# Sink values of the attention kept for all 128 rows, and their matmuls widened from 32 rows to 128

## The chip, the cores and the metric

The kernel runs on one core of one Trainium2 chip. The metric is the device time of one execution in microseconds (us); lower is better.

## The reference

The reference is a sliding-window attention with sink keys, followed by a feed-forward block. Sizes are 4 batches, 8 heads, 768 positions, head dimension 64, 4 sinks, window 128; then 3072 tokens, model width 512, feed-forward width 1024. Cut to what matters:

```python
keep = is_sink | in_window                       # key is among the first 4, or within the last 128
scores = np.where(keep, q @ k.T / sqrt(64), -1e9)
a = exp(scores - max); a = a / (a.sum() + 1e-9)
x = a @ v                                        # heads side by side: 3072 x 512
h = x @ w_in
solu = h * softmax(h)
ln = (solu - mean) / sqrt(var + 1e-6) * g_ln
out = ln @ w_out
```

## The kernel before, in words

Work goes by chunks of 128 queries: 6 chunks for a batch, 24 in all (`n` is the chunk, `c = n % 6` its place in the batch). Every float32 value is split into a high and a low part of a type (fp32r) that one pass of TensorE carries, so products are sums of two or three matmuls.

For each chunk the heads go in two blocks of 4 (`hb`) or in 4 pairs (`pr`). `turn_q`, `turn_k` (L415) transpose queries and keys on TensorE; `score` (L457, L458) makes the scores `s` of one head in two matmuls, in PSUM buffers of a pool with two (tag `s`, shared with those transposes); on VectorE `pick` (L464, COPY_PREDICATED) and `mask` (L474) take them out, `negate`, `invert` and `normalise` (L482, L494, L501) belong to the softmax; `turn_p` (L507) transposes the probabilities. `value` multiplies them with the values, pair by pair, into `acc` (shown as `av`): for each of the two heads a matmul over the chunk's own keys (L567) and one over the chunk before (L570), and, where `c` is not 0, one for the sinks of both heads (L573). There are thus 20 x 4 = 80 sink matmuls. `gather` (L580) sums the result on VectorE, `hidden` (L613) and `project` (L682) are the two feed-forward products, `turn_u` (L667) transposes between them, and `scale` (L687) and `store` write out through the buffers `ob` (two of them).

The sinks' probabilities of all 8 heads are brought together: `turn_sinks` transposes them to `skp`, whose 128 rows go by (head, high or low, sink), 16 rows a head and 32 a pair. `take_sinks` (L556) copies them twice to `skt`, once with the odd heads' rows set to zero and once with the even heads' rows, by the 0/1 columns `even` and `odd`. The sinks' values come once a batch into `vsraw` in the same order of rows; `sink_values` (L401 to L407, VectorE) splits them into high and low and puts them, in either order, in `vsink`. The sink matmul of pair `pr` takes rows 32*pr to 32*pr+31 of `vsink` (weights) and of `skt` (moving, 2 x 128 columns).

The order on every engine is fixed by a table, `PLAN`: for each step a number in sixteenths of a chunk's time. All steps of all chunks are sorted by `16*n + number` and issued in that order, each engine taking its own. `PLAN_W` does the same for the weights, which are split while the first chunks run. In the lists of order below, names end in the batch or chunk, then block or pair, then a serial number.

Of the kernel before, what the change touches and what calls it, by code (L numbers as in the profile page):

```python
# [10 lines left out]
F32 = mybir.dt.float32  # L11
F32R = mybir.dt.float32r
I32 = mybir.dt.int32
AF = mybir.ActivationFunctionType
ALU = mybir.AluOpType
# [31 lines left out]
    "sinks_lo": (-14.95, -12.0),  # L47
    "v_hi": (-31.65, -20.95),
    "v_lo": (-20.9, -18.8),
    "sink_values": (-34.95,),  # L50
    "turn_sinks": (-10.8,),
    "take_sinks": (-10.6,),
    "value": (-8.9, -8.2, -4.25, -1.4),
# [49 lines left out]
P = 128  # L103
# [39 lines left out]


def _outside(nc, consts, n_f, w_f):
    """Whether the two scalars leave the banded path's range."""
    ok = consts.tile([P, 4], F32, name="ok")
    nc.vector.tensor_scalar(ok[:, 0:1], n_f, 0.0, None, op0=ALU.is_ge)
    nc.vector.tensor_scalar(ok[:, 1:2], n_f, float(NSK), None, op0=ALU.is_le)
    nc.vector.tensor_scalar(ok[:, 2:3], w_f, 1.0, None, op0=ALU.is_ge)  # L150
    nc.vector.tensor_scalar(ok[:, 3:4], w_f, float(P), None, op0=ALU.is_le)
    allok = consts.tile([P, 1], F32, name="allok")
    nc.vector.tensor_reduce(allok, ok, axis=AX.X, op=ALU.min)
    general = consts.tile([P, 1], I32, name="general")
    nc.vector.tensor_scalar(general, allok, -1.0, 1.0, op0=ALU.mult, op1=ALU.add)
    return general


# High words of float64 whose numbers have float32's least and greatest exponent, as float32.
LEAST, MOST = struct.unpack("<2f", struct.pack("<2I", 0x38100000, 0x47EFFFFF))  # L160


def _banded(ctx, tc, q, k, v, n_sink, window, w_in, w_out, g_ln, out, val, wts):
    nc = tc.nc
    n_f, w_f = val[:, 0:1], val[:, 1:2]
    w1h, w1l, w2h, w2l = wts
    B, H, S, D = q.shape
# [3 lines left out]
    NPAIR = H // 2  # L171
# [7 lines left out]
    cpool = ctx.enter_context(tc.tile_pool(name="cpool", bufs=1))  # L179
    sb = ctx.enter_context(tc.tile_pool(name="sb", bufs=2))  # L180
# [26 lines left out]
                nc.sync.dma_start(g_sb, g_ln.rearrange("(kt p) -> p kt", p=P))  # L207

    def scalars(_, j):
        """The two int64 scalars on every partition, in float32 (exact where they can lie  # L210
        between two positions)."""
        nc.gpsimd.tensor_copy(words_f, words)
        lo, hi = words_f[:, :, 0], words_f[:, :, 1]
        nc.gpsimd.tensor_scalar(val, lo, 0.0, None, op0=ALU.is_lt)
        nc.gpsimd.tensor_tensor(val, val, hi, op=ALU.add)
        nc.gpsimd.tensor_scalar(val, val, 4294967296.0, None, op0=ALU.mult)
        nc.gpsimd.tensor_tensor(val, val, lo, op=ALU.add)

    # masks: query less key position, within a chunk (rel) and against the chunk before (rel + P)
    def at_least(out, x, lead):  # L220
        """x where lead * (partition less column) is at least (lead < 0), 0 elsewhere"""
        nc.gpsimd.affine_select(out, x, pattern=[[-lead, P]], compare_op=ALU.is_ge, fill=0.0,
                                base=-(lead < 0), channel_multiplier=lead)

# [16 lines left out]
    even = cpool.tile([P, 1], F32, name="even")  # L241
    odd = cpool.tile([P, 1], F32, name="odd")
    par = cpool.tile([P, NPAIR], F32, name="par")

    def masks(_, j):
        if j == 0:
            # a batch's first chunk
            nc.gpsimd.tensor_scalar(near, rel, w_f, None, op0=ALU.is_lt)
            at_least(near, near, 1)
            nc.gpsimd.tensor_scalar(old, ki, n_f, None, op0=ALU.is_lt)  # L250
            nc.gpsimd.tensor_copy(is_sink.rearrange("p g s -> p (g s)"), old[:, 0:NSK])
            nc.gpsimd.tensor_tensor(old, old, near, op=ALU.add)
            barred(bias0, old)
        elif j == 1:
            # the later ones
            nc.gpsimd.tensor_scalar(old, rel, float(P), w_f, op0=ALU.add, op1=ALU.is_lt)
            at_least(old, old, -1)
            nc.gpsimd.tensor_tensor(old, old, near, op=ALU.add)
            barred(bias1[:, 4:SEG], old)
            nc.gpsimd.tensor_scalar(far.rearrange("p g s -> p (g s)"), rel[:, 0:NSK], float(P), w_f,  # L260
                                    op0=ALU.add, op1=ALU.is_ge)
            nc.gpsimd.tensor_tensor(far, far, is_sink, op=ALU.mult)
            nc.gpsimd.tensor_copy(bias2[:, 4:SEG], bias1[:, 4:SEG])
            for t, bias in ((far, bias1), (is_sink, bias2)):
                barred(bias.rearrange("p (g s) -> p g s", s=4)[:, 0:SEG // 4 + 1:SEG // 4, :], t)
        else:
            ones = s_i[:, 0, :]
            nc.gpsimd.memset(ones, 1)
            at_least(m_cur, ones, 1)
            at_least(m_prev, ones, -1)  # L270
            # rows of the sink blocks go by (head, hi|lo, sink): which belong to even heads
            nc.gpsimd.memset(par, 1.0)
            nc.gpsimd.affine_select(par, par, pattern=[[-32, NPAIR]], compare_op=ALU.is_ge,
                                    fill=0.0, base=0, channel_multiplier=1)
            nc.gpsimd.affine_select(par, par, pattern=[[32, NPAIR]], compare_op=ALU.is_ge,
                                    fill=0.0, base=15, channel_multiplier=-1)
            nc.gpsimd.tensor_tensor(par[:, 0:2], par[:, 0:2], par[:, 2:4], op=ALU.add)
            nc.gpsimd.tensor_tensor(even, par[:, 0:1], par[:, 1:2], op=ALU.add)
            nc.gpsimd.tensor_scalar(odd, even, -1.0, 1.0, op0=ALU.mult, op1=ALU.add)
# [1 line left out]
    neg_half = cpool.tile([P, 1], F32, name="neg_half")  # L281
    nc.vector.memset(neg_half, -0.5)

    # weights, split into two parts that float32r products carry
    NB = 512
    blocks = [(w1h, w1l, w_in, kt, slice(i * NB, (i + 1) * NB)) for kt in range(KT1) for i in range(DFF // NB)]
    NW1 = len(blocks)
# [13 lines left out]
        bits = st["wbits", j] = sb.tile([P, NB], I32, tag=BIT_TAGS[j], name=f"wbits_{j}", bufs=2 + (BIT_TAGS[j] != "ob"))  # L301
        nc.scalar.activation(bits.bitcast(F32), raws[j][:, :, 1].bitcast(F32), AF.Abs)

    # float32 words of float64 ones: the sign and the exponent's first bit stay, the exponent's
    # other seven bits and the fraction's first 23 move up by three. What float32's exponents do
    # not reach goes to the nearest that they do.
    def least_w(_, j):
        t = st["wbits", j].bitcast(F32)
        nc.vector.tensor_scalar(t, t, LEAST, MOST, op0=ALU.max, op1=ALU.min)
# [27 lines left out]
        eng = nc.vector if j in LO_DVE else nc.gpsimd  # L337
        eng.tensor_tensor(wl[:, kt, cols], st["w", j], wh[:, kt, cols].bitcast(F32), op=ALU.subtract)  # L338

    # keys of four chunks: those at even positions of a batch before those at odd ones  # L340
    ring = cpool.tile([P, H, 4, SEG], F32R, name="ring")
    slot_of = (0, 2, 1, 3)
    st = {}
# [51 lines left out]
    def sink_values(n, _):  # L395
        b, c = divmod(n, NC)
        if c == 0:
            raw = st["vsraw", b]
            hi = sb.tile([P, D], F32R, tag="vshi", name=f"vshi_{b}", bufs=1)
            lo = sb.tile([P, D], F32R, tag="vslo", name=f"vslo_{b}", bufs=1)  # L400
            nc.vector.tensor_copy(hi, raw)  # L401
            nc.vector.tensor_tensor(lo, raw, hi.bitcast(F32), op=ALU.subtract)
            vk = sb.tile([P, 2, D], F32R, tag="vsink", name=f"vsink_{b}", bufs=2)
            tmp = sb.tile([P, 2, D], F32, tag="vstmp", name=f"vstmp_{b}", bufs=1)
            for i, (x, y) in enumerate(((hi, lo), (lo, hi))):
                nc.vector.tensor_scalar(tmp[:, i, :], y.bitcast(F32), odd, None, op0=ALU.mult)
                nc.vector.scalar_tensor_tensor(vk[:, i, :], x.bitcast(F32), even, tmp[:, i, :],  # L407
                                               op0=ALU.mult, op1=ALU.add)
            st["vsink", b] = vk

    def turn(n, hb, nm):
# [146 lines left out]
    def value(n, pr):  # L558
# [10 lines left out]
                lhs = st["vs", n - 1, hb][:, jp, 2 * x:2 * x + 2, :].rearrange("p t d -> p (t d)")  # L569
                nc.tensor.matmul(acc[:, x], lhs, pt[:, 2 * jp + x], start=False, stop=False)  # L570
        if not alone:
            rows = slice(32 * pr, 32 * pr + 32)
            nc.tensor.matmul(acc[:, :, 0, :], st["vsink", b][rows].rearrange("p t d -> p (t d)"),  # L573
                             st["skt", n][rows], start=False, stop=True)

    def gather(n, pr):
        hb, jp = divmod(pr, HB // 2)
# [9 lines left out]
        nc.sync.dma_start(ysh[D:P], y[0:D, :, 1, :])  # L587

    def tokens(n, hb):
        """x, heads side by side and tokens along the free axis."""  # L590
        y, ysh = st["y", n, hb], st["ysh", n, hb]
        xt = st["xt", n, hb] = sb.tile([P, HB // 2, P], F32, tag="xt", name=f"xt_{n}_{hb}", bufs=2)
        nc.gpsimd.tensor_tensor(xt[0:D], y[0:D, :, 0, :], ysh[0:D], op=ALU.add)  # L593
        nc.gpsimd.tensor_tensor(xt[D:P], y[D:P, :, 1, :], ysh[D:P], op=ALU.add)
# [37 lines left out]
    def solu(n, _):  # L632
# [1 line left out]
        su = sm.tile([P, 1], F32, tag="su", name=f"su_{n}")  # L634
        nc.vector.scalar_tensor_tensor(u, st["h", n], 1.0, st["e", n], op0=ALU.mult, op1=ALU.mult,
                                       accum_out=su)
        # eps times the square of the softmax's divisor: the divisor is taken into the root
        d = sm.tile([P, 1], F32, tag="d", name=f"d_{n}")
        nc.vector.tensor_scalar(d, st["se", n], EPS_SUM, None, op0=ALU.add)  # L639
        nmu = st["nmu", n] = sm.tile([P, 1], F32, tag="nmu", name=f"nmu_{n}")  # L640
# [48 lines left out]
    def store(n, _):  # L689
        nc.sync.dma_start(out[n * P:(n + 1) * P, :], st["ob", n])  # L690

    # When a chunk's steps are issued, in sixteenths of the time one chunk takes, from the
    # start of its first feed-forward product on; every engine takes its own in that order.
    stages = (load_k, load_q, load_v, k_hi, k_lo, q_hi, q_lo, turn_q, turn_k, take_q, swap_q, take_k, ring_sinks,
              score, pick, mask, negate, exps, invert, normalise, turn_p, p_hi, p_lo, part_new, part_old, sinks_hi, sinks_lo,
              v_hi, v_lo, sink_values, turn_sinks, take_sinks, value, gather, shift, tokens, x_hi, x_lo,
# [9 lines left out]


def _dense(ctx, tc, q, k, v, out, n_f, w_f, wts):
    """Any n_sink and window: every key of a sequence, in native float32 products."""
    nc = tc.nc  # L710
    B, H, S, D = q.shape
    w1h, w1l, w2h, w2l = wts
# [161 lines left out]
```

## Time and profile before

| What | Value |
|---|---|
| Time, median of 3 runs | 549.36 us (549.30 to 549.49) |
| Profiled execution, first to last instruction (span) | 547.0 us |
| Mean granted TensorE clock | 0.991 |
| Busy: TensorE matmul / weight loads | 491.5 us (90%) / 405.7 us (74%) |
| Busy: VectorE / ScalarE / GpSimd | 433.9 us (79%) / 372.3 us (68%) / 356.3 us (65%) |
| Sink matmuls (L573) | 80, from 72.0 to 518.4 us, 379 ns each |

Of the profiled execution the span is the only time that the page gives; the runs' median is 2.4 us above it. PE is TensorE's matmuls, PEld its weight loads, DVE VectorE, ACT ScalarE, POOL GpSimd, SP the engine that issues DMAs. A matmul's listed length is longer than the distance to the next one, since matmuls are pipelined: the start times tell what one costs the engine, not the lengths.

### The profile page before, as it was taken

Reading aid. Unit: us, or ns where it says so; the run is one execution under the profiler, and the core shown is the slowest. Engines: PE = TensorE matmul, PEld = TensorE weight load, DVE = VectorE, ACT = ScalarE, POOL = GpSimd, SP = SyncE. Lnnn points to the kernel's source line nnn. Section 1 sums busy time; section 2 is a strip of 40 time slices with the busy share of each in tenths; the row PEclk is TensorE's granted clock in tenths of the full one; section 3 lists DMA queues with packets and bytes.
Section 4 is the critical chain, followed back from the end, with each engine's and each line's share of the span. In section 5 each row is a group of like instructions: output and inputs, shape, how many; then the busy total and the mean of one; then the engine's idle time right before and its main releaser. Section 6 shows DMA issues by size and latency. Waiting matters only on the chain. (4 is left out here: it accounts for less than half of the span.)

```text
span 547.0 us, 9854 instructions
## 1 busy us (share of the span) xinstructions
PE 491.5 (90%) x2756; PEld 405.7 (74%) x2756; DVE 433.9 (79%) x1435; ACT 372.3 (68%) x1034; POOL 356.3 (65%) x510
## 2 busy tenths in 40 slices
PE   0046788999999999999999999999999999999995
PEld 0034566788788888888888888888888888888783
DVE  4999999986987787787887788788878878778531
ACT  3477867776676777677677677677768767755432
POOL 3967697896584677666675667667656757747520
PEclk9999898999999999999999999999999999999999
DMA  7777533343444543443444343343345343211111
GB/s 260 235 172 190 133 70 69 86 98 90 87 98 96 125 88 73 113 90 74 109 89 96 88 96 90 87 101 91 83 101 121 83 103 86 59 50 19 32 29 44
DMA packets 104205, 53.42 MB, mean 98 GB/s; under 512 B 80528, under 2 KB 92816, under 8 KB 104144
## 3 DMA queue, kind: packets, MB, share of 16 engines
q1 hardware_dynamic: 104144, 52.72, 39.9%
q8 instruction: 25, 0.41, 0.3%
q14 instruction: 36, 0.29, 0.2%
HBM read 27.53 MB, written 6.42 MB: 62 GB/s over the span
## 5 line engine op out<-in xcount | busy, mean ns | idle before, releaser
L602 POOL TENSOR_TENSOR xl<-xt,xh 128x256 fp32r<-128x256 f32 x48 | 35.5, 740 | 79.6 <-ACT xh L598 79.5
L613 PE MATMUL h<-w1h,xh 128*128 128x512 f32 x192 | 86.6, 451 | 0.2 <-DVE d L639 0.2
L489 ACT ACTIVATE sc<-sc,nmx 128x136 f32<-128x136 f32 (+1 forms) x192 | 76.3, 404 | 8.7 <-DVE nmx L482 8.7
L682 PE MATMUL o<-w2h,uh 128*128 128x512 f32 x192 | 80.1, 417 | 0.3 <-ACT uh L671 0.3
L613 PE MATMUL h<-w1l,xh 128*128 128x512 f32 x192 | 76.3, 398 | 0.2 <-DVE w1l L338 0.2
L613 PE MATMUL h<-w1h,xl 128*128 128x512 f32 x192 | 76.3, 398 | 0.0
L682 PE MATMUL o<-w2h,ul 128*128 128x512 f32 x192 | 75.7, 394 | 0.0
L682 PE MATMUL o<-w2l,uh 128*128 128x512 f32 x192 | 75.5, 393 | 0.0
L501 DVE TENSOR_SCALAR sc<-sc,rs 128x136 f32<-128x136 f32 (+1 forms) x192 | 75.3, 453 | 0.0
L580 DVE TENSOR_REDUCE y<-av 128x256 f32<-128x512 f32 x96 | 65.5, 683 | 6.2 <-PE av L573 5.8
L457 PE MATMUL s<-ring,qT 128*128 128x264 f32 (+1 forms) x192 | 57.5, 308 | 14.4 <-DVE mx L474 12.5
L522 POOL TENSOR_SCALAR_AFFINE_SELECT pc<-pt 128x1024 fp32r<-128x1024 f32 x40 | 44.5, 1111 | 23.7 <-DVE pt L515 23.7
L464 DVE COPY_PREDICATED s<-m_cur,s 128x128 f32<-128x128 int32 x96 | 26.4, 292 | 38.7 <-PE s L458 38.0
L474 DVE CUSTOM_DVE_ANT_0 sc<-s,bias 128x136 f32<-128x136 f32 (+1 forms) x192 | 50.6, 290 | 6.0 <-PE s L458 5.8
L457 PEld LDWEIGHTS s<-ring,qT 128*128 128x128 f32 x192 | 37.9, 198 | 23.2 <-issue 7.2
L458 PE MATMUL s<-ring,qX 128*128 128x264 f32 (+1 forms) x192 | 55.0, 295 | 0.0
L415 PE MATMUL qt<-ident_r,qs 128*128 128x128 f32 x192 | 26.3, 263 | 30.8 <-POOL qs L369 29.5
L425 ACT CAST qT<-qt 128x512 fp32r<-128x512 f32 x48 | 28.1, 586 | 34.6 <-PE qt L415 34.6
L593 POOL TENSOR_TENSOR xt<-y,ysh 64x256 f32<-64x256 f32 x48 | 35.4, 737 | 19.4 <-DVE s L464 11.4
L415 PEld LDWEIGHTS qt<-ident_r,qs 128*128 128x128 f32 x192 | 19.9, 145 | 36.4 <-POOL qs L369 30.7
L528 POOL TENSOR_SCALAR_AFFINE_SELECT pt<-pt 128x1024 fp32r<-128x1024 f32 x40 | 44.7, 1118 | 1.5
L567 PE MATMUL av<-pc,vs 128*128 128x256 f32 x160 | 45.5, 307 | 0.2
(124 smaller groups left out, 1434.7 us busy)
## 6 DMA issues: line engine op xcount, KB each, us to landing
qX<-qT SPq DMA_DIRECT2D x96, 128.0 KB, 2.3
qn<-in_q_dram SPq DMA_DIRECT2D x24, 256.0 KB, 3.3
kn<-in_k_dram SPq DMA_DIRECT2D x24, 256.0 KB, 3.3
vn<-in_v_dram SPq DMA_DIRECT2D x24, 256.0 KB, 3.2
ysh<-y SPq DMA_DIRECT2D x96, 64.0 KB, 2.1
out_dram<-ob SPq DMA_DIRECT2D x24, 256.0 KB, 2.9
wraw<-in_moe_w_in_dram SPq DMA_DIRECT2D x8, 512.0 KB, 7.2
wraw<-in_moe_w_out_dram SPq DMA_DIRECT2D x8, 512.0 KB, 3.8
```

The costliest lines, as they stand in the source:

```text
L415: nc.tensor.transpose(tr[:, j, :], sp[:, j, :, :].rearrange("p t d -> p (t d)"), ident_r)
L457: nc.tensor.matmul(o, st["qT", n, hb][:, j, :], rhs, start=True, stop=False)
L458: nc.tensor.matmul(o, st["qX", n, hb][:, j, :], rhs, start=False, stop=True)
L474: nc.vector.tensor_tensor_reduce(out=st["sc", n, hb][:, j, c0:c1], in0=st["s", n, h].rearrange("p a x -> p (a x)")[:, c0:c1], in1=bias0 if ...
L489: nc.scalar.activation(sc[:, i, c0:c1], sc[:, i, c0:c1], AF.Exp, bias=nmx[:, i:i + 1], scale=1.0, accum_out=ssum[:, i:i + 1])
L501: nc.vector.tensor_scalar(sc[:, j, c0:c1], sc[:, j, c0:c1], rs[:, j:j + 1], None, op0=ALU.mult)
L522: nc.gpsimd.affine_select(pc, pt.bitcast(F32), pattern=[[0, HB * 2], [1, P]], compare_op=ALU.is_ge, fill=0.0, base=0, channel_multiplier=-1)
L528: nc.gpsimd.affine_select(pt, pt.bitcast(F32), pattern=[[0, HB * 2], [-1, P]], compare_op=ALU.is_ge, fill=0.0, base=-1, channel_multiplier=1)
L567: nc.tensor.matmul(acc[:, x], lhs, pc[:, 2 * jp + x], start=(x == 0), stop=(alone and x == 1))
L580: nc.vector.tensor_reduce(st["y", n, hb][:, jp], st["acc", n, pr].rearrange("p x s q -> p x q s"), axis=AX.X, op=ALU.add)
L613: nc.tensor.matmul(st["h", n][:, cols], a[:, kt % 2, :], w[:, kt, cols], start=(kt == 0 and m == 0), stop=(kt == KT1 - 1 and m == 2))
L682: nc.tensor.matmul(st["o", n], a[:, kt % 4, :], w[:, kt, :], start=(kt == 0 and m == 0), stop=(kt == KT2 - 1 and m == 2))
```

## The change

`vsink` now holds, for each of the 4 pairs, a copy of the batch's sink values over all 128 rows in which only that pair's 32 rows are kept and the others are zero. A 0/1 table `mine` (128 x 4, made once on GpSimd) says which rows are whose. The sink matmul then takes all 128 rows of that copy and all 128 rows of `skt`. `sink_values` issues one more VectorE instruction a batch (the multiplication by `mine`, 128 x 512), takes its scratch space from a buffer `ob` instead of buffers of its own, has one buffer for `vsink` instead of two, and stands at -12.0 in the table instead of -34.95. Comments were removed, so lines shift by 3 to 5.

```diff
-    "sink_values": (-34.95,),
+    "sink_values": (-12.0,),
...
+    mine = cpool.tile([P, NPAIR, 1], F32, name="mine")
...
+            nc.gpsimd.affine_select(mine[:, :, 0], par, pattern=[[32, NPAIR]], compare_op=ALU.is_ge,
+                                    fill=0.0, base=31, channel_multiplier=-1)
...
-            hi = sb.tile([P, D], F32R, tag="vshi", name=f"vshi_{b}", bufs=1)
-            lo = sb.tile([P, D], F32R, tag="vslo", name=f"vslo_{b}", bufs=1)
+            four = sb.tile([P, 8, D], F32R, tag="ob", name=f"vsx_{b}", bufs=2)
+            hi, lo, tmp = four[:, 0, :], four[:, 1, :], four[:, 2:4, :].bitcast(F32)
...
-            vk = sb.tile([P, 2, D], F32R, tag="vsink", name=f"vsink_{b}", bufs=2)
-            tmp = sb.tile([P, 2, D], F32, tag="vstmp", name=f"vstmp_{b}", bufs=1)
+            vk = sb.tile([P, NPAIR, 2 * D], F32R, tag="vsink", name=f"vsink_{b}", bufs=1)
             for i, (x, y) in enumerate(((hi, lo), (lo, hi))):
                 nc.vector.tensor_scalar(tmp[:, i, :], y.bitcast(F32), odd, None, op0=ALU.mult)
-                nc.vector.scalar_tensor_tensor(vk[:, i, :], x.bitcast(F32), even, tmp[:, i, :],
+                nc.vector.scalar_tensor_tensor(tmp[:, i, :], x.bitcast(F32), even, tmp[:, i, :],
                                                op0=ALU.mult, op1=ALU.add)
+            nc.vector.tensor_tensor(vk, tmp.rearrange("p t d -> p (t d)").unsqueeze(1).to_broadcast([P, NPAIR, 2 * D]),
+                                    mine.to_broadcast([P, NPAIR, 2 * D]), op=ALU.mult)
...
-            rows = slice(32 * pr, 32 * pr + 32)
-            nc.tensor.matmul(acc[:, :, 0, :], st["vsink", b][rows].rearrange("p t d -> p (t d)"),
-                             st["skt", n][rows], start=False, stop=True)
+            nc.tensor.matmul(acc[:, :, 0, :], st["vsink", b][:, pr, :], st["skt", n], start=False, stop=True)
```

TensorE's order does not change. VectorE's does, in four places, one a batch. Batch 1's sink values before (`vshi_1`, `vslo_1`, `vstmp_1`, `vsink_1` are their buffers) stand ahead of chunk 5's last softmax steps:

```order
L620 TENSOR_REDUCE mx2_3_1780<-h_3_1600 128x1 x2
L401 CAST vshi_1_1809<-vsraw_1_1553 128x64
L402 TENSOR_TENSOR vslo_1_1810<-vsraw_1_1553,vshi_1_1809 128x64
L406 TENSOR_SCALAR vstmp_1_1814<-vslo_1_1810,odd_110 128x64
L407 SCALAR_TENSOR_TENSOR vsink_1_1813<-vshi_1_1809,even_109,vstmp_1_1814 128x64
L406 TENSOR_SCALAR vstmp_1_1814<-vshi_1_1809,odd_110 128x64
L407 SCALAR_TENSOR_TENSOR vsink_1_1813<-vslo_1_1810,even_109,vstmp_1_1814 128x64
```

With the change the seven instructions (scratch `vsx_1`) stand behind the sum of chunk 5's last pair (`av_5_3`, L583) and between the scores of heads 3 and 5 of chunk 7:

```order
L583 TENSOR_REDUCE y_5_1_2127<-av_5_3_2132 128x256
...
L479 ISA sc_7_0_2165,mx_7_0_2166<-s_7_3_2193,bias1_103 128x136
L479 ISA mx_7_0_2166 128x1
L404 CAST vsx_1_2224<-vsraw_1_1554 128x64
L405 TENSOR_TENSOR vsx_1_2224<-vsraw_1_1554,vsx_1_2224 128x64
L408 TENSOR_SCALAR vsx_1_2224<-vsx_1_2224,odd_110 128x64
L409 SCALAR_TENSOR_TENSOR vsx_1_2224<-vsx_1_2224,even_109 128x64
L408 TENSOR_SCALAR vsx_1_2224<-vsx_1_2224,odd_110 128x64
L409 SCALAR_TENSOR_TENSOR vsx_1_2224<-vsx_1_2224,even_109 128x64
L412 TENSOR_TENSOR vsink_1_2227<-vsx_1_2224,mine_112 128x512
L469 COPY_PREDICATED s_7_5_2233<-m_cur_105,s_7_5_2233 128x128
```

The group moved by about one and a half chunks and grew by the instruction on L412. Batch 0's group moves in the same way, within the stretch in which the weights (`wbits`) are split. Before, it stands ahead of chunk 0's first scores:

```order
L322 SCALAR_TENSOR_TENSOR wbits_8_224<-wraw_8_201,wbits_8_224 128x512
L401 CAST vshi_0_308<-vsraw_0_257 128x64
...
L407 SCALAR_TENSOR_TENSOR vsink_0_312<-vslo_0_309,even_109,vstmp_0_313 128x64
L317 SCALAR_TENSOR_TENSOR wbits_10_236<-wraw_10_226,wbits_10_236 128x512
L309 TENSOR_SCALAR wbits_11_321<-wbits_11_321 128x512
L474 ISA sc_0_0_337,mx_0_0_338<-s_0_2_318,bias0_102 128x128
```

Now it stands within chunk 1's scores:

```order
L479 ISA mx_1_0_483 128x1
L325 SCALAR_TENSOR_TENSOR wbits_12_383<-wraw_12_325,wbits_12_383 128x512
L404 CAST vsx_0_515<-vsraw_0_259 128x64
...
L409 SCALAR_TENSOR_TENSOR vsx_0_515<-vsx_0_515,even_109 128x64
L412 TENSOR_TENSOR vsink_0_518<-vsx_0_515,mine_112 128x512
L469 COPY_PREDICATED s_1_5_524<-m_cur_105,s_1_5_524 128x128
```

The copy of head 5's scores out of PSUM now comes behind the seven in both places.

## The prediction

> **What bounds the kernel now.** I read the page's first two parts first, then the busy time by stage, then who waits for whom. The page's share of busy time and its slices:
>
> ```profile
> PE 491.5 (90%) x2756; PEld 405.7 (74%) x2756; DVE 433.9 (79%) x1435; ACT 372.3 (68%) x1034; POOL 356.3 (65%) x510
> PE   0046788999999999999999999999999999999995
> DVE  4999999986987787787887788788878878778531
> ```
>
> TensorE is full from slice 8 to the end, and before that VectorE is. The windows by stage put numbers on it (columns: PE, PEld, DVE, ACT and POOL busy us with instruction counts, clock, DMA share, GB/s):
>
> ```profile
> 60.00:80.00 20.00, 16.37 (x93) 13.31 (x93) 19.93 (x61) 15.41 (x48) 16.45 (x21) 0.93 0.48 102
> 80.00:100.00 20.00, 16.85 (x94) 13.48 (x92) 19.54 (x60) 15.51 (x44) 16.06 (x21) 0.91 0.36 79
> 440.00:460.00 20.00, 20.00 (x118) 16.70 (x117) 15.94 (x58) 14.26 (x43) 14.06 (x20) 1.00 0.40 93
> ```
>
> Up to 100 us VectorE is busy 19.93 and 19.54 of 20 us and TensorE is not full; later TensorE is busy 20.00 of 20 at clock 1.00 and VectorE 15.94. Matmul lengths are modelled, so I check with the waits between 100 and 520 us, of PE and then of DVE:
>
> ```profile
> PE ptp L507 <- DVE sc L501: 0.2, 1, 0.2
> DVE s L464 <- PE s L458: 58.7, 64, 1.4
> DVE y L580 <- PE av L573: 5.8, 19, 2.0
> DVE sc L474 <- PE s L458: 5.6, 9, 1.4
> DVE mx L620 <- PE h L613: 4.6, 8, 1.4
> ```
>
> In 420 us TensorE waits 0.2 us for others, while VectorE waits 74.7 us for TensorE (58.7 + 5.8 + 5.6 + 4.6). From 100 us on the time is TensorE's own issue, so a matmul that costs it less shortens the run until another engine falls behind.
>
> **What a sink matmul costs TensorE now.** It stands in the trace 80 times, 6 before 99.4 us (where VectorE bounds) and 74 after:
>
> ```profile
> L573 PE MATMUL av<-skt,vsink x6: 377/379/383, 72.0 to 93.3; 32*128 32x256 f32 x6
> L573 PE MATMUL av<-skt,vsink x74: 376/379/383, 99.5 to 518.4; 32*128 32x256 f32 x74
> ```
>
> The cost is read from start times. One sink matmul with a feed-forward product behind it, in the timeline of PE:
>
> ```profile
> 285.44 0.39 PE L682 MATMUL o<-w2h,ul 128*128 128x512 f32 x1
> 285.68 0.28 PE L567 MATMUL av<-pc,vs 128*128 128x256 f32 x1
> 285.79 0.28 PE L570 MATMUL av<-pt,vs 128*128 128x256 f32 x1
> 285.91 0.28 PE L567 MATMUL av<-pc,vs 128*128 128x256 f32 x1
> 286.03 0.28 PE L570 MATMUL av<-pt,vs 128*128 128x256 f32 x1
> 286.23 0.38 PE L573 MATMUL av<-skt,vsink 32*128 32x256 f32 x1
> 286.54 0.50 PE L682 MATMUL o<-w2h,uh 128*128 128x512 f32 x1
> 286.88 0.40 PE L682 MATMUL o<-w2l,uh 128*128 128x512 f32 x1
> 287.12 0.39 PE L682 MATMUL o<-w2h,ul 128*128 128x512 f32 x1
> ```
>
> A 128-row matmul of 256 columns is followed by the next after 0.12 us (285.91 to 286.03), one of 512 after 0.24 (286.88 to 287.12). Around the sink matmul the steps are 0.20 before it (286.03 to 286.23), 0.31 behind it and 0.34 for the first product after: 0.85 where 0.12 + 0.12 + 0.24 = 0.48 would do. The weight loads say why:
>
> ```profile
> 285.91 0.19 PEld L570 LDWEIGHTS av<-pt,vs 128*128 128x128 f32 x1
> 286.23 0.18 PEld L573 LDWEIGHTS av<-skt,vsink 32*128 32x128 f32 x1
> 286.54 0.19 PEld L682 LDWEIGHTS o<-w2h,uh 128*128 128x128 f32 x1
> 286.65 0.19 PEld L682 LDWEIGHTS o<-w2l,uh 128*128 128x128 f32 x1
> ```
>
> L570's weights load at 285.91, one matmul ahead of it (286.03). The sink's load at 286.23 together with its own matmul, and so do those of the product behind it (286.54); only then does loading ahead resume. Twice the pipeline runs empty, when TensorE goes from 128 rows to 32 and back. The excess is 0.85 - 0.48 = 0.37 us. With other matmuls behind it:
>
> ```profile
> 253.50 0.28 PE L570 MATMUL av<-pt,vs 128*128 128x256 f32 x1
> 253.71 0.38 PE L573 MATMUL av<-skt,vsink 32*128 32x256 f32 x1
> 254.02 0.38 PE L567 MATMUL av<-pc,vs 128*128 128x256 f32 x1
> 254.24 0.28 PE L570 MATMUL av<-pt,vs 128*128 128x256 f32 x1
> 281.06 0.28 PE L570 MATMUL av<-pt,vs 128*128 128x256 f32 x1
> 281.26 0.38 PE L573 MATMUL av<-skt,vsink 32*128 32x256 f32 x1
> 281.58 0.54 PE L415 MATMUL qt<-ident_r,qs 128*128 128x128 f32 x4
> ```
>
> Before the next pair: 253.50 to 254.24 is 0.74 where three steps of 0.12 would take 0.36, so 0.38. Before transposes: 281.06 to 281.58 is 0.52 for two steps, where 0.24 would do, so 0.28; what the first transpose loses is not in these rows and I leave it out.
>
> Here the Trainium skill has two rules that go apart. "TensorEngine Tiling (Array Packing)", Key Properties, says that a change of tiling mode, from all rows to 32, drains the engine; by it the 0.37 us go away. "TensorE: Matmul & The Clock Gate", in its table of goals, says that a small-K matmul takes the same time as one with K=128, so that widening gains nothing; that is the second rival below. The rows above agree with the first as far as they go.
>
> **The change part by part.**
> - *Sink matmuls on 128 rows.* The nearest rows are L567 and L570: 128 rows, 256 columns, 0.12 us. I take that, with no emptying. From 99.4 us on, TensorE's order has 33 of the 74 ahead of transposes L415 and 41 ahead of other work: 33 x 0.28 + 41 x 0.37 = 9.2 + 15.2 = 24.4 us. The 6 early ones give at most 6 x 0.38 = 2.3 us; I count none, since VectorE sets the pace there.
> - *One more VectorE instruction a batch*, 128 x 512 from SBUF. Nearest rows are the like subtractions:
>
> ```profile
> L675 DVE TENSOR_TENSOR ul<-utp,uh x48: 676/684/692, 97.3 to 536.6; 128x512 fp32r<-128x512 f32 x48
> L338 DVE TENSOR_TENSOR w1l<-wbits,w1h x4: 874/927/1776, 20.5 to 75.4; 128x512 fp32r<-128x512 f32 x4
> ```
>
>   L338 has all operands in SBUF, as this one has, so 0.93 us; ends 0.68 and 1.78. In batch 0 it falls where VectorE is full: +0.9 us (0.7 to 1.8).
> - *The group moved.* Batch 3's six instructions now:
>
> ```profile
> 380.86 0.75 DVE L401 CAST vshi<-vsraw 128x64 fp32r<-128x64 f32 x1
> 383.30 0.28 DVE L407 SCALAR_TENSOR_TENSOR vsink<-vslo,even,vstmp 128x64 fp32r<-128x64 f32 x1
> ```
>
>   That is 2.7 us, with the seventh 3.6. Batch 0's move changes no sum, as VectorE is full in both places. In batches 1 to 3 the copy of head 5's scores (L469) now stands behind it, and TensorE waits for that copy when it wants a score buffer for the head after next. The cover is VectorE's waiting, 74.7 us in 420, or 3.6 us in a chunk (about 20 us: 22 chunks lie between the first sink matmul of chunk 1, at 72.0 us, and those of chunk 23, the last at 518.4), and the second buffer. If the cover is whole it costs 0; if gone, 3.6 us each. Between these I take the row of TensorE waiting for the same copies where VectorE is full, before 100 us, 12.5 us in 9 waits or 1.4 each, and halve it to 0.7, since VectorE is not full here: 3 x 0.7 = 2.1 us (0 to 10.8).
>
> ```profile
> PE s L457 <- DVE mx L474: 12.5, 9, 2.5
> ```
>
> - *One `vsink` buffer.* The seventh instruction must wait for the last sink matmul of the batch before. On VectorE it stands behind the sum of that very pair (`av_5_3`), which waits for that matmul anyway: 0. *Scratch in `ob`.* VectorE waits for the store of chunk 2, a whole chunk earlier: 0; chunk 4's `ob` follows chunk 3's, whose store is some ten sixteenths older: 0. In the start the split of weight block 13 takes block 10's buffer, not block 5's: ScalarE starts it at 63.47 us, and POOL's last reading of block 10 starts at 51.70 and takes 1.29, 10 us earlier: 0; without this cover it would cost what the weights come late.
>
> ```profile
> 51.70 1.29 POOL L338 TENSOR_TENSOR w2l<-wbits,w2h 128x512 fp32r<-128x512 f32 x1 [0.38 <-ACT w2h L333]
> 63.47 0.67 ACT L302 ACTIVATE wbits<-wraw 128x512 f32<-128x512 f32 x1
> ```
>
> - *One POOL instruction for `mine`*, 128 x 4, within the first 4 us, long before TensorE's first work: 0. No DMA is added, and SP's queue keeps its order.
>
> Sum: -24.4 + 0.9 + 2.1 = -21.4 us. The profiled span of 547.0 us becomes 525.6. The median is 2.4 us above that span; nothing shows the rest changing, so 549.4 - 21.4 = 528.0 us.
>
> Without any cost behind it, and with the early six, the gain is 26.7 us, or 522.7. With the upper ends (1.8 + 10.8) it is 11.8, or 537.6. My range for this case is 522.5 to 533.5; the upper end gives back half of the possible 10.8 us.
>
> **The rivals.**
> - *VectorE becomes the bound.* A chunk loses 4 sink excesses, 1.31 us in the steady order (2 x 0.28 + 0.37 + 0.38); VectorE's 3.6 us of waiting shrink to 2.3, and in-order waits eat that in places. If half of the gain comes back as TensorE waiting for score copies, the time is 549.4 - 10.7 = 538.7, or 534 to 543. For it: the burst of 3.6 us is longer than those 2.3. Against: 0.2 us of waits now.
> - *The emptying doesn't come from the 32 rows.* L573 is also the only matmul here that writes two separate runs of 128 columns, and no 128-row matmul does so in the trace. If that is the cause, the 0.20 and 0.31 stay and only VectorE's work is added: 549.4 + 0.9 + 2.1 = 552.4, slower. The mean excess now is 24.4 / 74 = 0.33 us, and the additions are 3.0 / 74 = 0.04 us for each: the run gets slower once a widened sink matmul still loses over 0.29 us. If the additions are hidden too, it is 549.4, no change. Against: the weight load is held back as well, and it doesn't write.
>
> **How the numbers follow.** The forecast, 528.0, gets 0.84, VectorE as the bound 0.09, and no effect of the rows 0.07, of which 0.04 end slower and 0.03 within 0.2% (1.1 us, about what a measurement of this kernel tells from no change). Faster is 0.84 + 0.09 = 0.93. The range 522.5 to 533.5 leaves out the rivals, 0.16, and little of its own case.
>
> **What the profile after would show.** L577 (the sink) at 0.12 us from its neighbours, its weights loaded one matmul ahead, and a listed length near L567's 0.28: right; steps of 0.20 and 0.31 still there: the second rival. PE waiting for DVE at the scores, from 100 us on: up to 3 us as forecast, over 8 the first rival. The seventh instruction, L412, near 0.9 us. What would make me wrong most simply is a burst in front of the score copies that TensorE waits out in full, or a start stretched by more than the 0.9 us.

## The result and the profile after

The changed kernel takes 535.02 us in the median of 4 runs (533.91 to 537.25), against 549.33 us before: a ratio of 0.975, 95% interval 0.9724 to 0.9775. It is 14.3 us faster, where 21.4 us was forecast, and the time lies above the range of 522.5 to 533.5 us. The profiled execution took 535.71 us, with a span of 534.0.

The page's busy time, and one steady window (PE, PEld, DVE, ACT, POOL busy us with instruction counts, clock, DMA share, GB/s):

```profile
PE 471.1 (88%) x2756; PEld 403.3 (76%) x2756; DVE 448.8 (84%) x1439; ACT 375.5 (70%) x1034; POOL 356.2 (67%) x511
440.00:460.00 20.00, 20.00 (x127) 17.59 (x126) 17.16 (x59) 14.94 (x44) 14.86 (x22) 1.00 0.40 103
```

TensorE is still full in a steady stretch, and 127 matmuls fall into these 20 us where 118 did before (not all the same ones). The sink matmuls by the source line, then one of them in the timelines of PE and of its weight loads:

```profile
L577 PE MATMUL av<-skt,vsink x80: 280/282/415, 75.2 to 505.3; 128*128 128x256 f32 x80
267.89 0.28 PE L575 MATMUL av<-pt,vs 128*128 128x256 f32 x1
268.01 0.28 PE L577 MATMUL av<-skt,vsink 128*128 128x256 f32 x1
268.13 0.28 PE L572 MATMUL av<-pc,vs 128*128 128x256 f32 x1
...
267.89 0.19 PEld L577 LDWEIGHTS av<-skt,vsink 128*128 128x128 f32 x1
```

The steps are 0.12 us on both sides, where they were 0.20 and 0.31, the weights load one matmul ahead (267.89 against 268.01), and the listed length is that of its neighbours. So the widening does what the forecast said. What it did not say is in the waits of PE between 100 and 520 us (waiting instruction, releaser: us in all, times, longest), and in two windows by stage:

```profile
PE s L462 <- DVE mx L479: 6.0, 4, 1.9
285.50:288.50 3.00, 1.11 (x9) 0.94 (x8) 2.89 (x13) 1.12 (x6) 0.00 (x0) 1.00 0.04 14
288.50:292.50 4.00, 3.99 (x19) 3.34 (x19) 3.96 (x17) 2.98 (x10) 2.96 (x5) 0.57 0.23 54
```

TensorE waits 6.0 us for score buffers, where all its waits were 0.2 us before. By the prediction's signs that is neither the forecast (up to 3 us) nor the first rival (over 8 us). In one such place it is busy 1.11 of 3 us, and in the 4 us after that its granted clock is 0.57. The same place in the timelines, of DVE, POOL and PE:

```profile
283.32 0.59 DVE L404 CAST vsx<-vsraw 128x64 fp32r<-128x64 f32 x1
283.95 0.81 DVE L405 TENSOR_TENSOR vsx<-vsraw,vsx 128x64 fp32r<-128x64 f32 x1
284.79 0.75 DVE L408 TENSOR_SCALAR vsx<-vsx,odd 128x64 f32<-128x64 f32 x1
285.57 0.28 DVE L409 SCALAR_TENSOR_TENSOR vsx<-vsx,even 128x64 f32<-128x64 f32 x1
285.77 0.25 DVE L408 TENSOR_SCALAR vsx<-vsx,odd 128x64 f32<-128x64 f32 x1
286.06 0.28 DVE L409 SCALAR_TENSOR_TENSOR vsx<-vsx,even 128x64 f32<-128x64 f32 x1
286.38 0.69 DVE L412 TENSOR_TENSOR vsink<-vsx,mine 128x512 fp32r<-128x512 f32 x1
286.99 0.29 DVE L469 COPY_PREDICATED s<-m_cur,s 128x128 f32<-128x128 int32 x1
...
283.13 0.73 POOL L596 TENSOR_TENSOR xt<-y,ysh 64x256 f32<-64x256 f32 x1 [3.17 <-DMA ysh<-y]
283.94 0.74 POOL L597 TENSOR_TENSOR xt<-y,ysh 64x256 f32<-64x256 f32 x1
284.75 0.74 POOL L372 TENSOR_TENSOR ks<-kn,ks 128x256 fp32r<-128x256 f32 x1
...
285.49 0.28 PE L462 MATMUL s<-ring,qT 128*128 128x264 f32 x1
285.61 0.28 PE L463 MATMUL s<-ring,qX 128*128 128x264 f32 x1
287.77 0.36 PE L462 MATMUL s<-ring,qT 128*128 128x264 f32 x1 [1.89 <-DVE mx L479]
```

The seven VectorE instructions of `sink_values` run from 283.32 to the copy at 286.99, 3.67 us. That copy (L469, head 5's scores) and the mask after it free the buffer for the next score: TensorE starts it at 287.77, 2.16 us after the matmul before, where 0.12 is the step. That is a hole of 2.04 us, and the profile has one like it in each of batches 1 to 3 (2.02, 2.04 and 2.01 us), while in the start TensorE falls behind too.

### The profile page after: what moved, and what is told of

It reads as the page before. It is cut to its first block, busy times and chain, and to the rows that moved or that the text cites. A ratio compares the mean times of both kernels' runs of the same rounds, so it can differ in the third digit from the quotient of the medians.

```text
span 534.0 us, 9856 instructions
## 1 busy us (share of the span) xinstructions
PE 471.1 (88%) x2756; PEld 403.3 (76%) x2756; DVE 448.8 (84%) x1439; ACT 375.5 (70%) x1034; POOL 356.2 (67%) x511
## 5 line engine op out<-in xcount | busy, mean ns | idle before, releaser
L462 PE MATMUL s<-ring,qT 128*128 128x264 f32 (+1 forms) x192 | 60.4, 320 | 20.6 <-DVE mx L479 18.5
L685 PE MATMUL o<-w2h,uh 128*128 128x512 f32 x192 | 78.0, 406 | 0.2 <-ACT uh L674 0.2
L583 DVE TENSOR_REDUCE y<-av 128x256 f32<-128x512 f32 x96 | 65.4, 682 | 3.5 <-PE av L577 3.2
L463 PE MATMUL s<-ring,qX 128*128 128x264 f32 (+1 forms) x192 | 56.6, 300 | 0.1
L420 PE MATMUL qt<-ident_r,qs 128*128 128x128 f32 x192 | 24.2, 254 | 30.4 <-POOL qs L372 29.3
L420 PEld LDWEIGHTS qt<-ident_r,qs 128*128 128x128 f32 x192 | 21.3, 148 | 31.2 <-POOL qs L372 30.5
L572 PE MATMUL av<-pc,vs 128*128 128x256 f32 x160 | 43.8, 295 | 0.0
L463 PEld LDWEIGHTS s<-ring,qX 128*128 128x128 f32 x192 | 39.5, 206 | 4.9 <-issue 0.3
L616 PEld LDWEIGHTS h<-w1h,xl 128*128 128x128 f32 x192 | 36.5, 190 | 8.5
```

Of the source, the lines that this page charges most:

```text
L420: nc.tensor.transpose(tr[:, j, :], sp[:, j, :, :].rearrange("p t d -> p (t d)"), ident_r)
L462: nc.tensor.matmul(o, st["qT", n, hb][:, j, :], rhs, start=True, stop=False)
L463: nc.tensor.matmul(o, st["qX", n, hb][:, j, :], rhs, start=False, stop=True)
L572: nc.tensor.matmul(acc[:, x], lhs, pc[:, 2 * jp + x], start=(x == 0), stop=(alone and x == 1))
L583: nc.vector.tensor_reduce(st["y", n, hb][:, jp], st["acc", n, pr].rearrange("p x s q -> p x q s"), axis=AX.X, op=ALU.add)
L616: nc.tensor.matmul(st["h", n][:, cols], a[:, kt % 2, :], w[:, kt, cols], start=(kt == 0 and m == 0), stop=(kt == KT1 - 1 and m == 2))
```

## The experiments

My theory, "burst": the block of seven in front of a score copy costs TensorE what it is longer than the slack of that place, four times, and the rest is the clock after a hole. The rival, "no slack": VectorE is too full for the shorter chunk, wherever the block stands. Each kernel below is set against the kernel before in its own comparison; that kernel's median was 548.32 us in the first four, 549.35 in the next three and 549.26 in the last, so a difference between two experiments can be off by 1 us.

**The block without the widening.** Sink matmuls on 32 rows, all else as in the change:

```diff
-            nc.tensor.matmul(acc[:, :, 0, :], st["vsink", b][:, pr, :], st["skt", n], start=False, stop=True)
+            rows = slice(32 * pr, 32 * pr + 32)
+            nc.tensor.matmul(acc[:, :, 0, :], st["vsink", b][rows, pr, :], st["skt", n][rows], start=False, stop=True)
```

> Everything of the change but the wide matmul: sink matmuls take 32 rows of the pair's copy again, the seven VectorE instructions stay where the change put them. Theory 'burst' (the seven in front of head 5's score copy make TensorE wait about 2 us in each of batches 1 to 3, about 3 us are lost in the start, and a hole can be followed by 3.4 us at half clock): 549.3 + 3 x 2.0 + 2.6 + up to 3.4 = 558 to 561 us. Rival 'no slack' (VectorE only falls behind because TensorE got faster): 549 to 552 us, no holes over 1 us at those places.

Measured: 557.59 us (556.97 to 558.64), ratio 1.0172 (1.0147 to 1.0197), against 548.32 for the kernel before in that comparison: 9.3 us slower. In the waits of PE after 100 us and the timeline of one hole:

```profile
PE s L462 <- DVE mx L479: 4.4, 3, 1.5
417.85 0.28 PE L463 MATMUL s<-ring,qX 128*128 128x264 f32 x1
419.60 0.36 PE L462 MATMUL s<-ring,qT 128*128 128x264 f32 x1 [1.46 <-DVE mx L479]
```

Three holes stand in the same places, though the sink matmuls take 32 rows again; they are some 1.6 us long (419.60 less the matmul before at 417.85 and a step of 0.12), and no half-clock stretch follows them in this profile, whose clock is 1.00 from 100 to 540 us. The time is a little under the band, but the band was reckoned from 549.3 us and this comparison's kernel before is 1 us faster; the extra 9.3 us lies within the 8.7 to 11.7 us that the band stands for. The verdict is for "burst": the block costs on its own.

The holes are 0.4 us shorter than in the changed kernel because the block is. In the timelines of DVE and POOL, its first instruction, the copy behind it, and GpSimd's instruction at its start:

```profile
415.55 0.19 DVE L404 CAST vsx<-vsraw 128x64 fp32r<-128x64 f32 x1
418.81 0.29 DVE L469 COPY_PREDICATED s<-m_cur,s 128x128 f32<-128x128 int32 x1
...
414.96 0.73 POOL L597 TENSOR_TENSOR xt<-y,ysh 64x256 f32<-64x256 f32 x1 [3.74 <-DVE s L469]
```

The block takes 3.26 us here, since its first instruction takes 0.19 us where it took 0.59 above; the other six take 0.25 to 0.80 us, within 0.01 us of the rows above. 3.26 - 1.63 and 3.67 - 2.04 both leave 1.63 us of the block that TensorE does not feel, the cover of the place.

**No block in batches 1 to 3.** Batch 0's values serve for all, so the kernel leaves out the sink values of the other batches:

```diff
-        if c == 0:
+        if c == 0 and b > 0:
+            st["vsink", b] = st["vsink", 0]
+        elif c == 0:
```

> The changed kernel with the group of seven in batch 0 only; batches 1 to 3 use batch 0's sink values, so their part of the output is left out. 'burst': three holes of 2.0 us and up to two half-clock stretches (1.7 us each) go, 535.0 - 6.0 - 3.4 = 525.6 us (524 to 528). 'no slack': the holes turn up at other score copies, 531 to 535 us.

Measured: 527.36 us (526.84 to 528.02), ratio 0.9614 (0.959 to 0.9637). The waits of PE after 100 us fall to 0.4 us at the scores: the shorter chunk by itself makes no holes. As the run also takes the three blocks' work off VectorE, it does not say where that work could stand; but with the run before, which has the holes without the shorter chunk, "no slack" falls.

```profile
PE s L464 <- DVE mx L481: 0.4, 1, 0.4
```

**The block on GpSimd**, in the same place of the table, the same values in seven instructions:

```diff
-            nc.vector.tensor_copy(hi, raw)
-            nc.vector.tensor_tensor(lo, raw, hi.bitcast(F32), op=ALU.subtract)
+            nc.gpsimd.tensor_copy(hi, raw)
+            nc.gpsimd.tensor_tensor(lo, raw, hi.bitcast(F32), op=ALU.subtract)
...
-            nc.vector.tensor_tensor(vk, tmp.rearrange("p t d -> p (t d)").unsqueeze(1).to_broadcast([P, NPAIR, 2 * D]),
+            nc.gpsimd.tensor_tensor(vk, tmp.rearrange("p t d -> p (t d)").unsqueeze(1).to_broadcast([P, NPAIR, 2 * D]),
```

> The changed kernel with the same group at the same place in the table, but on GpSimd (seven instructions, same values). 'burst': holes gone and VectorE relieved in the start too, 525.6 less 2 to 3 us: 522 to 526 us. 'no slack': 531 to 535 us. A third way: GpSimd's longer stay holds up queries and keys (its transposes L420 wait), 528 to 533 us with TensorE waiting for GpSimd.

Measured: 524.66 us (523.75 to 526.2), ratio 0.9569 (0.9539 to 0.9598), 10.4 us below the change, or 9.4 when each is set against its own kernel before (23.7 - 14.3). TensorE waits for scores 0.6 us after 100 us, and for GpSimd not at all there:

```profile
PE ptp L513 <- DVE sc L507: 0.6, 2, 0.3
PE s L463 <- DVE mx L480: 0.6, 2, 0.4
PE o L686 <- ACT uh L675: 0.2, 1, 0.2
```

**The seven spread** over seven places of the table, all on VectorE:

```diff
-    "sink_values": (-12.0,),
+    "sink_values": (-20.58, -13.93, -12.02, -10.82, -9.78, 3.34, 4.1,),
```

> The changed kernel with the seven VectorE instructions given seven places of the table (-20.58 to 4.1) in place of one; the same VectorE work. 'burst' (the length of the block in front of a score copy counts, not the sum): 524 to 528 us. 'no slack' (the sum counts): 532 to 535 us.

Measured: 531.05 us (528.94 to 532.19), ratio 0.9682 (0.9645 to 0.9719). It lies between the two bands, so neither reading had it right. The holes shrink to about 0.5 us each, 3.1 us of waits in seven pieces, but TensorE loses more in the start than with the block on GpSimd: before 100 us it waits 13.1 us for score buffers, against 7.7 us there.

```profile
PE s L470 <- DVE mx L487: 3.1, 7, 0.5
```

So the length of the block counts after 100 us, and spreading it in these places is a partial cure.

**The widening alone.** As on GpSimd above, with 32 rows again:

> The group on GpSimd as in e3_pool, and sink matmuls on 32 rows again. With e3_pool it gives the widening alone, without the block on VectorE. If the 24.4 us of the forecast hold (74 x 0.33): 524.7 + 24.4 = 549 us (547 to 551). If widening is worth less than its start times say (TensorE waits for others in the shorter chunk): 540 to 546 us. GpSimd's group costs nothing here only if this run is within 0.3% of the kernel before.

Measured: 549.08 us over 10 runs, the kernel before 549.35 over 13, ratio 0.9996 (0.9985 to 1.0006). With GpSimd's block the rest of the change costs nothing that this comparison can tell, and the widening is 549.08 - 524.66 = 24.4 us, or 23.4 when each is set against its own kernel before (23.7 - 0.3).

**64 rows instead of 32.** As on GpSimd, the matmul's rows cut to those of two pairs:

```diff
-            nc.tensor.matmul(acc[:, :, 0, :], st["vsink", b][:, pr, :], st["skt", n], start=False, stop=True)
+            rows = slice(64 * (pr // 2), 64 * (pr // 2) + 64)
+            nc.tensor.matmul(acc[:, :, 0, :], st["vsink", b][rows, pr, :], st["skt", n][rows], start=False, stop=True)
```

> e3_pool with each sink matmul on 64 rows (those of two pairs; the copy is zero in the other pair's rows). If any height below 128 empties TensorE's pipeline, the steps around the matmul stay 0.20 and 0.31 and the time is e6's, 547 to 551 us. If the cost goes with the rows left out, half of it: about 536 us. If only 32 rows do it: 525 us.

Measured, in a single run: 548.31 us. The timelines of PEld and PE:

```profile
285.17 0.28 PE L576 MATMUL av<-pt,vs 128*128 128x256 f32 x1
285.38 0.18 PEld L579 LDWEIGHTS av<-skt,vsink 64*128 64x128 f32 x1
285.38 0.38 PE L579 MATMUL av<-skt,vsink 64*128 64x256 f32 x1
285.69 0.50 PE L687 MATMUL o<-w2h,uh 128*128 128x512 f32 x1
286.02 0.40 PE L687 MATMUL o<-w2l,uh 128*128 128x512 f32 x1
```

The steps are 0.21, 0.31 and 0.33 us, 0.85 in all as with 32 rows, and the weights again load together with their matmul: 64 rows cost what 32 did. It is the change of height that empties the pipeline, not the number of rows left out. By the Trainium skill, "TensorEngine Tiling (Array Packing)", Key Properties, every change of tiling mode drains the engine; the trace agrees: 0.37 us over the 0.48 without it, for 32 rows and for 64.

**A longer block.** The changed kernel with the multiplication by `mine` three times:

```diff
-            nc.vector.tensor_tensor(vk, tmp...
+            for _ in range(3):
+                nc.vector.tensor_tensor(vk, tmp...
```

> The changed kernel with the multiplication by mine issued three times in place of once, the same values: the block on VectorE is 1.2 us longer in each batch. 'burst' with the cover used up: each of the three holes grows from 2.0 to 3.2 us, the start's by 1.2: 535.0 + 4.8 = 539.8 us, 538 to 542 with more half-clock stretches. If the holes of 2.0 us come from something else of that place (its waits, not its length): 535 to 537 us.

Measured: 543.89 us (543.16 to 544.1), 8.9 us above the change, more than either band. In the timelines of DVE and PE:

```profile
170.86 0.59 DVE L404 CAST vsx<-vsraw 128x64 fp32r<-128x64 f32 x1
173.90 2.15 DVE L413 TENSOR_TENSOR vsink<-vsx,mine 128x512 fp32r<-128x512 f32 x3
175.96 0.29 DVE L470 COPY_PREDICATED s<-m_cur,s 128x128 f32<-128x128 int32 x1
...
173.16 0.28 PE L464 MATMUL s<-ring,qX 128*128 128x264 f32 x1
176.75 0.36 PE L463 MATMUL s<-ring,qT 128*128 128x264 f32 x1 [3.31 <-DVE mx L480]
```

The hole is now 176.75 - 173.16 - 0.12 = 3.47 us behind a block of 175.96 - 170.86 = 5.10 us, which leaves 1.63 us once more; all four places grew by 1.4 to 1.5 us, 5.8 in all, where 1.2 each was expected (the repeats start 0.72 us apart). The cover is used up, one for one. The two profiled executions lie 8.0 us apart (543.68 against 535.71), so 2.2 us are left in them for something else. The clock fits in kind: the windows behind the first and second of the later holes have means of 0.57 and 0.52:

```profile
177.00:181.00 4.00, 4.00 (x22) 3.71 (x21) 3.83 (x16) 3.44 (x11) 2.59 (x4) 0.57 0.08 20
293.00:300.00 7.00, 6.31 (x25) 5.54 (x26) 6.11 (x27) 5.13 (x17) 2.96 (x5) 0.52 0.20 47
```

The clock's record in this profile has half clock for 3.4 us behind the first and third of the later holes and for 6.8 us behind the second, 13.6 us, where the change's has 6.8. If half clock loses half of that time, it is 3.4 us more; that is an estimate, and more than the 2.2 us that are left.

**One short instruction left on VectorE**, at another place; the other six stay on GpSimd (the edit is shown against the kernel with the block on GpSimd):

```diff
-    "sink_values": (-12.0,),
+    "sink_values": (-12.0, -6.0),
...
-            nc.gpsimd.tensor_tensor(vk, tmp...
+            nc.vector.tensor_tensor(vk, tmp...
```

> e3_pool with only the multiplication by mine back on VectorE, at -6.0 in the table, one instruction of 0.7 us a batch; the other six stay on GpSimd. 'burst' with a cover (a block costs TensorE only what it exceeds the slack of its place by, some 1.6 us where the change put it): no new hole over 0.3 us, 523 to 526 us, the same as e3_pool. If every microsecond on VectorE costs one (no cover at all): 524.7 + 3 x 0.7 + the start = 527 to 528 us.

Measured: 524.03 us (523.6 to 524.41), ratio 0.9537 (0.9521 to 0.9553): like the block on GpSimd, and the fastest kernel of this study. Its waits at the scores are 0.4 us in all after 100 us. So 0.7 to 0.9 us of VectorE a batch can be free. The slack of this other place was not worked out, so the run does not test the rule of the slack by itself.

## Why the prediction was wrong, point by point

- *TensorE bounds the time, so a cheaper matmul shortens it.* Right.
- *The sink matmul's excess, 24.4 us.* Right: the widening alone measured 23.4 to 24.4 us. That the upper figure is the forecast's to the tenth is luck. The second rival (the emptying comes from the two runs of output) is out: the widened matmul writes the same runs at steps of 0.12 us.
- *The new VectorE instruction, 0.93 us.* It took 0.69. Right within its ends.
- *The group moved, 3 x 0.7 us, and the start, 0.9 us.* This is the step that failed. The sum had 2.1 us for the three moves, which cost 6.1, 0.9 us for the start, which cost 2.0, and nothing for the clock; the change lies 9.4 to 10.4 us above the kernel with the block on GpSimd, and the block alone cost 9.3 us. Between the profiled executions of the change and of the GpSimd kernel there are 11.1 us. The three holes are the 6.1; in the start TensorE is 2.0 us behind at its 301st matmul, which starts as follows in the change, with the block on GpSimd, and before the change:

```profile
109.23 0.40 PE L685 MATMUL o<-w2h,uh 128*128 128x512 f32 x1
...
107.27 0.40 PE L686 MATMUL o<-w2h,uh 128*128 128x512 f32 x1
...
107.03 0.39 PE L682 MATMUL o<-w2h,uh 128*128 128x512 f32 x1
```

  The two stretches of 3.4 us at half clock behind two of the holes would lose 1.7 us each if half clock loses half of the time, which is an estimate. That makes 11.5 us, near the 11.1.
- *Why the start cost 2.0, not 0.9.* "Batch 0's move changes no sum" is wrong: the first three of the block took longer in the new place. In the timeline of DVE, before the change and after it:

```profile
35.17 0.18 DVE L401 CAST vshi<-vsraw 128x64 fp32r<-128x64 f32 x1
35.38 0.23 DVE L402 TENSOR_TENSOR vslo<-vsraw,vshi 128x64 fp32r<-128x64 f32 x1
35.64 0.25 DVE L406 TENSOR_SCALAR vstmp<-vslo,odd 128x64 f32<-128x64 f32 x1
...
54.58 0.71 DVE L404 CAST vsx<-vsraw 128x64 fp32r<-128x64 f32 x1
55.32 0.68 DVE L405 TENSOR_TENSOR vsx<-vsraw,vsx 128x64 fp32r<-128x64 f32 x1
56.03 0.61 DVE L408 TENSOR_SCALAR vsx<-vsx,odd 128x64 f32<-128x64 f32 x1
```

  They take 2.00 us where they took 0.66. With L412's 0.69 that is 2.0 us more on an engine that is full there, and TensorE's 301st matmul starts at 109.2 us where it started at 107.0 before.
- *Why 0.7 was too little.* I took half of a wait from another stretch, though the trace of before had the slack of the very place. In its timelines of DVE and PE, in chunk 7:

```profile
172.66 0.29 DVE L464 COPY_PREDICATED s<-m_cur,s 128x128 f32<-128x128 int32 x1 [1.36 <-PE s L458]
173.29 0.08 DVE L474 DVE_READ_ACCUMULATOR2_ANT mx<- 128x1 f32 x1
173.63 0.29 PE L457 MATMUL s<-ring,qT 128*128 128x264 f32 x1
```

  VectorE waits 1.36 us ahead of head 5's copy, and from the end of its mask (173.29 + 0.08) to the score that takes the buffer (173.63) are 0.26 us. The cover is 1.62 us. The block of 3.67 us exceeds it by 2.05: the measured hole. The blocks of 3.26 and 5.10 us in the experiments give 1.64 and 3.48, where 1.63 and 3.47 were measured. So TensorE waits out what exceeds the cover, and not the whole block. Even the forecast's own 3.6 us would have given 2.0 each, 6 us for three, and 532 us. The average of 3.6 us of waiting in a chunk was no cover, since most of it lies elsewhere.
- *The first rival* (VectorE as the bound, at the score copies) named the place and, in its remark on the burst, the mechanism; the shorter chunk is not the cause, as the block alone shows the holes too. The prediction's last sentence named a burst and a longer start as what would make it wrong, though TensorE does not wait the burst out in full.
- *`ob`, one `vsink` buffer, GpSimd's `mine`: 0.* With 32 rows and GpSimd's block the ratio to the kernel before is 0.9996 (0.9985 to 1.0006), so nothing else of the change costs anything that these runs can tell.

## What to carry to other kernels

Here a matmul on fewer rows than its neighbours emptied TensorE's pipeline twice; filling the unused rows with zeros took 0.3 us a piece out of a stream that TensorE bounds. What prepares the zeros must not stand in one block in front of a copy that frees a PSUM buffer: compare the block's length with the slack at that place, which is the wait ahead of the copy plus the time from its end to the matmul that takes the buffer, and not with a mean of idle time. In these runs the work was free on an engine with time to spare (GpSimd), and with one short instruction of it on VectorE at another place.

## What the runs showed of the hardware

Three of the seven VectorE instructions take far longer than their size says. L404, L405 and L408 above end at 283.91, 284.76 and 285.54 us, each 0.05 to 0.08 us after a GpSimd instruction ends (283.86, 284.68, 285.49), and the same L408 takes 0.25 us when GpSimd is idle. By the Trainium skill, "SBUF — State Buffer", in the section on SBUF's two separate sides, VectorE and GpSimd share a pair of ports; a GpSimd instruction, or a VectorE one of certain kinds, that starts first holds it for its whole length, and the other waits. These rows agree: GpSimd's three start at 283.13, 283.94 and 284.75 us, each ahead of VectorE's (283.32, 283.95, 284.79). About 1.5 us of the 3.67 went there (0.59 + 0.81 + 0.75 against 0.18 + 0.23 + 0.25 in the start of the kernel before). The run with 32 rows shows what that is worth for one of the three: its L404 starts late in GpSimd's instruction (415.55 us, in one from 414.96 to 415.69), ends 0.05 us after it as in the changed kernel, and so takes 0.19 us; block and hole are shorter by 0.4 us. What the hole would be without all three was not tried.

Half clock came with holes of 2.04 us (two of three in the changed kernel's profile) and of 3.5 us (three of three with the longer block), and not with those of 1.6 us. One profile of each does not give a threshold. The four runs of the change order by their clock: 533.91 and 534.33 us at 0.990, 535.71 at 0.985, 537.25 at 0.972. Those with the block in batch 0 alone do not (527.09 us at 0.981, 528.02 at 0.991), so the mean clock of a run by itself does not give its time.
